# Fused attention and FFN on one core: all attention ahead of the first FFN product, with shared x and operand tiles

## The chip, the core and the metric

The kernel runs on one core of a Trainium2 chip. The core has a matrix engine (TensorE, PE in the profile, with its weight loads listed as PEld), a vector engine (VectorE, DVE), a scalar engine (ScalarE, ACT) and a queue that here only starts transfers (SyncE, SP). Matmuls write to PSUM, eight banks of 512 fp32 numbers on each of 128 partitions; all else lives in SBUF, 128 partitions wide. The metric is the device time of one execution in microseconds, the median of several runs. A profile is one execution recorded by the hardware.

## The reference

Attention with a sigmoid in place of the softmax, whose result is the input of a two-layer FFN with a leaky ReLU:

```python
def _attn_ref(q, k, v):                     # each 8 x 12 x 448 x 64, fp32
    S = q.shape[2]
    scale = 1.0 / np.sqrt(q.shape[-1])
    scores = scale * np.matmul(q, k.transpose(0, 1, 3, 2)) - np.log(S)
    attn = 1.0 / (1.0 + np.exp(-scores))
    return np.matmul(attn, v).astype(np.float32)

def _moe_ref(x, w_in, w_out):               # x: 3584 x 768, w_in: 768 x 2048, w_out: 2048 x 768
    h = x @ w_in
    g = np.maximum(0.01 * h, h)
    return (g @ w_out).astype(np.float32)
```

`x` is the attention output with its heads side by side. `moe_w_in` and `moe_w_out` come as float64 bits, read by the kernel as pairs of int32.

## The kernel before, in words

**Units of work.** A *pair* is two heads of one batch: 8 x 6 = 48 pairs, `pairs[0]` to `pairs[47]`. `scores(h)` does two of four chunks of keys (three matmuls for each chunk and head, since q and k are split into a high and a low fp32r part) and gives them to ScalarE's sigmoid; `attn_v(0)` and `attn_v(1)` multiply by v; `keep` copies the result from PSUM to a third of an `x` tile of [128, 3, 448]. A pair is of one of three kinds (`part`, line 42): kind 0 cuts its 448 keys into four chunks of 112; kinds 1 and 2 form a *couple*, each with three chunks of 128 keys and 64 keys left, and those last 64 of both lie in one tile, so that four 64 x 64 matmuls of attn·v for the two pairs stand where two times two of 112 rows did. Before, 22 couples and 4 pairs of kind 0 (`JOINT_ALONE`, `JOINT`, lines 36 and 37).

**The FFN.** Both products use a seven-product scheme: `ORDER = 0, 1, 4, 5, 3, 6, 2` (line 20). A *quarter* q is two batches, 12 pairs, four `x` tiles. From them come seven operands (`Operands`, line 435): x0, x1, two of them after sums in place (`s3`, `sum1`, `sum4`), and one sum tile s2. Each operand is split in a high part (cast on ScalarE) and a low part (subtraction on VectorE). The first product of a quarter (`First`, line 520) runs over eight units u and the seven operands: 56 *steps*, each nine matmuls of 128x128 by 128x448. After some steps `after` evacuates and sums PSUM on ScalarE and VectorE and stores the results g to DRAM. The second product, from line 743, reads g back.

**Weights.** `prep` (line 249) rebuilds 16 blocks of weights (eight of w_in, eight of w_out) on VectorE: for each piece five integer instructions, at the end four subtractions, then two stores to DRAM. It is a generator; `prepare(q)` advances it by `PACES` yields at each slot. The first four blocks come in two pieces of 128x768, through tiles of the operands' pool `so`, the others in four pieces of 128x384. `advance(t)` (line 501) handles the first product's prepared weights, four groups for each unit: load into one of three `stage` tiles up to eight steps ahead and at most three groups beyond the last low part, high part three steps ahead, low part two steps ahead.

**The order around the change.** Nearly all instructions are pinned to the order in which the program issues them, engine by engine. The program runs in *slots*: `later(n, f)` puts f into the slot n ahead, and `slot(work)` issues the chores of the slot, then its work. Quarter 0's pairs run alone (lines 639 to 658). Then, for q = 1 to 3, the first product of quarter q-1 runs with quarter q's 12 pairs inserted between its steps (lines 663 to 678): scores(0) of pair i, attn·v of pair i-1, scores(1) of pair i. The last quarter's product runs alone (line 686). `PLAN` and `PLAN_ALONE` (lines 483 to 490) say in which slot the operands' parts are made: "e5.0" is the first slot of the quarter's pair 5, "p50" step 50 of the quarter before, "np0" step 0 of its own product; "h002" is the high part of operand 0, thirds 0 to 2, "l" a low part, "s" a sum.

**Space.** Operands have eight tiles with room for both parts (`so`), x and s2 five (`xp`). In PSUM the scores have three double banks in quarter 0, two afterwards; attn·v has two banks; while product and pairs are mixed, the first product has one bank for `px` and one for `pz`. When it runs alone at the end it has three of each. Tiles of v come from the weights' `ring` for pairs 0 to 8 and from a pool of their own afterwards.

Of the kernel before, what the change touches and what calls it, by code (L numbers as in the profile page):

```python
# [26 lines left out]
ALONE = 4  # L27


PACES = 1.45, 2.45, 1.46  # L30
LATER = 4
IDLE = 7
WAIT = 2, 7


JOINT_ALONE = 1, 3, 5, 7
JOINT = 0, 2, 4, 6, 8, 10
PER = 12
AHEAD_OF = 3
# [19 lines left out]
def attn_ffn_kernel(ctx: ExitStack, tc: tile.TileContext, qk, v, w_in, w_out, out):  # L59
# [17 lines left out]
    KR = S // NK  # L77
# [9 lines left out]
    td = [[tc.dram_tile([P, NOP, HW], F32, name=f"t{w}_{u}") for u in range(NU)] for w in range(2)]  # L87
    gd = [[tc.dram_tile([P, NU, S], F32, name=f"g_{p}_{n}") for n in range(NOP)] for p in range(NQ)]
# [160 lines left out]
    def prep():  # L249
# [3 lines left out]
        pieces = [(m, k, 4 if m >= ALONE else 2) for m in range(len(todo)) for k in range(4 if m >= ALONE else 2)]  # L253
        raws = []

        def load():
            at = len(raws)
            if at == len(pieces):
                return
            m, k, n = pieces[at]  # L260
            w, u = todo[m]
            size = 4 * HW // n
            pool = (so, "so", 2 * NB * S, NOP + 1) if m < ALONE else (pp, "wr", 2 * HW, 3)
# [4 lines left out]
        load()  # L268
        load()
        yield  # L270
        for at, (m, k, n) in enumerate(pieces):
# [3 lines left out]
            if m < ALONE - 1:  # L275
                load()
            elif (m, k) == (ALONE - 1, 1):
                for _ in range(3):
                    load()
# [15 lines left out]
            if m >= ALONE:  # L295
                load()
                yield
# [11 lines left out]
            yield from (None for _ in range(WAIT[m >= ALONE]))  # L309
# [4 lines left out]
    def prepare(q):  # L314
        nonlocal credit
        credit += PACES[0] if q == 0 else PACES[1] if (0, NU - 1) not in prepared else PACES[2]
        while credit >= 1:
            next(preps, None)
            credit -= 1

    xs = {}

    HALVES = slice(0, S // 2), slice(S // 2, S)
    OTHERWISE = 9

    class Pair:
# [6 lines left out]
        def load_qk(self):  # L333
            self.raw = raws.tile([P, 2, S], F32, tag="qk", name=f"qk_{self.i}")
            if self.i == 0:

                for cols in HALVES:
                    dma_act(out=self.raw[:, 0, cols], in_=qk[self.i, :, 0, cols])
                    dma(out=self.raw[:, 1, cols], in_=qk[self.i, :, 1, cols])
            elif self.i == 1:  # L340
                dma_act(out=self.raw[:, 0], in_=qk[self.i, :, 0])
                dma(out=self.raw[:, 1], in_=qk[self.i, :, 1])
            else:
                dma(out=self.raw, in_=qk[self.i])

        def load_v(self):
            rows, n = ((KR, 2 * NK), (P, 2 * NK - 2), (P, 2 * NK))[self.part]
            if self.i < OTHERWISE:
                t = ring.tile([P, 4 * HW], F32, tag="ring", name=f"v_{self.i}")
                self.v = t[:, :2 * NK * D].rearrange("p (a b) -> p a b", a=2 * NK)  # L350
            else:
                self.v = raws.tile([P, 2 * NK, D], F32, tag="v", name=f"v_{self.i}", bufs=2)
            dma(out=self.v[:rows, :n], in_=v[self.i, :rows, :n])
# [8 lines left out]
        def split(self):  # L362
# [5 lines left out]
            for n, cols in enumerate(HALVES):  # L368
# [6 lines left out]
        def scores(self, h):  # L375
            todo, acts = [], []
            for c in range(2 * h, 2 * h + 2):
                ps = psum_s(self.i * NK + c, f"sc_{self.i}_{c}")

                if self.part == 0:  # L380
                    k0, n, rows = c * KR, KR, slice(0, KR)
                elif c < NK - 1:
# [26 lines left out]
        def attn_v(self, h):  # L409
            if h == 0:  # L410
                self.pv = psum_v("pv", f"pv_{self.i}")
            rows = slice(0, P if self.part else KR)
            for c in range(2 * h, 2 * h + 2):
                if self.part and c == NK - 1:
                    continue
                for j, me in enumerate(heads):
                    mm(self.pv[me, :S], lhsT=self.v[rows, (NK - 1 if self.part else NK) * j + c, :], rhs=self.a[c][rows, j],
                       start=c == 0, stop=c == NK - 1, skip_group_check=True)
            if h == 1 and self.part == 2:
# [5 lines left out]
                later(1, x.keep, first=True)  # L425
            if h == 1 and self.part != 1:
                later(1, self.keep, first=True)

        def keep(self):
            half, c = divmod(self.i, NB)  # L430
            if c == 0:
                xs[half] = xp.tile([P, NB, S], F32, tag="x", name=f"x_{half}")
            copy(out=xs[half][:, c], in_=self.pv[:, :S])

    class Operands:
# [3 lines left out]
        def __init__(self, p):  # L439
            self.p, self.t, self.s2 = p, {}, None  # L440
# [9 lines left out]
        def high(self, n, a=0, b=NB):  # L450
            if n not in self.t:
                self.t[n] = so.tile([P, 2, NB, S], F32R, tag="so", name=f"so{n}_{self.p}")
            copy(out=self.t[n][:, 0, a:b], in_=self.of(n)[:, a:b])

        def low(self, n, a=0, b=NB):
            sub(self.t[n][:, 1, a:b], self.of(n)[:, a:b], self.t[n][:, 0, a:b])

        def s3(self):
            sub(self.x(0), self.x(0), self.x(2))

        def sum2(self, a, b):
            if self.s2 is None:
                self.s2 = xp.tile([P, NB, S], F32, tag="x", name=f"s2_{self.p}")
            sub(self.s2[:, a:b], self.x(3)[:, a:b], self.x(0)[:, a:b])

        def sum1(self, a, b):
            add(self.x(2)[:, a:b], self.x(2)[:, a:b], self.x(3)[:, a:b])

        def sum4(self, a, b):
            sub(self.x(1)[:, a:b], self.x(1)[:, a:b], self.s2[:, a:b])  # L470

        def do(self, what):
# [3 lines left out]
            if kind == "s":  # L476
                self.s3() if n == 3 else (self.sum1 if n == 1 else self.sum2 if n == 2 else self.sum4)(a, b)
            else:
                (self.high if kind == "h" else self.low)(n, a, b)

    PLAN = {
# [3 lines left out]
    PLAN_ALONE = {  # L487
# [32 lines left out]
    class First:  # L520
# [6 lines left out]
        def step(self):  # L527
# [10 lines left out]
            x = self.ops.t[n]  # L538
            for kk in range(NB):
                parts_mm(acc, w, slice(kk * P, kk * P + P), x[:, 0, kk], x[:, 1, kk], first and kk == 0, kk == NB - 1)  # L540
# [38 lines left out]
    per = 2 * NP  # L579
# [5 lines left out]
    zeros = st.tile([P, S], F32, tag="st", name="zeros", bufs=ST)[:, :S // 4]  # L585
# [12 lines left out]
    first, ops = None, None  # L598
    psv = ExitStack()
    psum_v = banks("ps_v", dict(pv=(2, 1)), psv)  # L600
    psum_two = banks("ps_s", dict(s0=(1, 2), s1=(1, 2)), psv)
    psum = banks("ps_a", dict(s2=(1, 2)))

    def psum_s(n, name):

        if n < per * NK:
            return (psum if n % 3 == 2 else psum_two)(f"s{n % 3}", name)
        return psum_two(f"s{n % 2}", name)

    def next_parts(i, *slots, how=None):  # L610

        if i + 2 <= last:
            later(slots[0], lambda: pairs[i + 2].high(how))
            later(slots[1], pairs[i + 2].low)
        if i + 4 <= last:
            later(slots[2], pairs[i + 4].load_qk)

    def go(q, where, work, busy=False):


        for x, plan, key in ((ops, PLAN, where), (before, PLAN if q > 1 else PLAN_ALONE, "n" + where)):
            if x is not None:
# [210 lines left out]
```

## Time and profile before

| | us |
|---|---|
| median of 3 runs | 1105.76 (1105.23 to 1106.14) |
| the profiled execution | 1105.26 |
| its span, first to last instruction | 1103.5 |
| PE busy | 1094.4 |
| VectorE busy | 669.2 |
| ScalarE busy | 614.5 |
| mean granted TensorE clock | 0.998 of full speed |

The profile's names follow the program: `sc` are scores, `s` the sigmoid's results, `pv` attn·v in PSUM, `qk` and `qks` a pair's q and k and their parts, `so` operands, `wx`, `w` a staged weight and its parts, `px_h`, `py_h`, `pz_h` the first product's accumulators, the same with `_o` the second's, `wr`, `wd`, `ws` preparation of weights, `c_h` results of the first product. A row of the time line has start, length, engine, line, operation, output<-input, shapes and the number of instructions; in brackets stands the idle time before it and what ended it. Since every helper issues through one line, L92 says little, and the tile names tell the work. A row of a group has the busy time, the mean length of one in ns, and the idle time in front. A row of a stage has the busy time of PE, PEld, VectorE, ScalarE and GpSimd with the number of instructions, then the clock, the DMA engines' busy share and GB/s. Matmuls are pipelined, so the end of one overlaps the start of the next, and starts are more exact than lengths.

### The profile page before, as it was taken

To read this page: it belongs to the slowest core of one execution; us is meant where nothing else is said; L and a number is where in the kernel's file an instruction comes from. 1 tells how busy PE (TensorE), PEld (TensorE's weight loads), DVE (VectorE), ACT (ScalarE), POOL (GpSimd) and SP (SyncE) were. 2 spreads that over 40 slices of the span, in tenths; PEclk is the share of its full clock that TensorE was granted. 3 is DMA by queue.
4 is the path that set the end of the run, shared out by engine and by line. 5 is a ranking of instruction groups with operands and counts; after the bars stand their busy time and mean duration, and the time that the engine had idled before them with its cause. 6 is when DMAs were issued, how large, how long until landed. Compare 5 with 4: busy or idle time off the path is not lost.

```text
span 1103.5 us, 16033 instructions
## 1 busy us (share of the span) xinstructions
PE 1094.4 (99%) x5978; PEld 898.2 (81%) x5978; DVE 669.2 (61%) x998; ACT 614.5 (56%) x866; POOL 0.3 (0%) x5
## 2 busy tenths in 40 slices
PE   9998999999999999999999999999999999999998
PEld 5556777777777777777778999999999999999998
DVE  5888888668776678676568766565433333343332
ACT  7886676678666667665657555554333232323331
POOL 0000000000000000000000000000000000000000
PEclk9999999999999999999999999999999999999999
DMA  7966988885888876787755989777645554454452
GB/s 275 336 216 221 329 294 295 283 280 157 276 255 284 262 243 218 237 284 243 253 192 163 297 275 292 267 276 226 204 146 145 156 184 145 131 182 147 156 153 89
DMA packets 105422, 250.11 MB, mean 227 GB/s; under 512 B 11712, under 2 KB 55232, under 8 KB 105344
## 3 DMA queue, kind: packets, MB, share of 16 engines
q1 hardware_dynamic: 104912, 248.62, 68.5%
q8 instruction: 47, 0.77, 0.3%
q10 hardware_dynamic: 432, 0.46, 0.1%
q14 instruction: 31, 0.25, 0.1%
HBM read 164.63 MB, written 84.41 MB: 226 GB/s over the span
## 4 chain that ended last, share of the span: by engine, by line
PE 94%; DVE 3%; ACT 1%; DMA 1%; issue 1%; ACTq 0%; SPq 0%; DVEq 0%
PE px_h L92 21%; PE px_o L92 21%; PE pv L92 11%; PE pz_o L92 10%; PE pz_h L92 10%; PE sc L92 10%; PE py_h L92 5%; PE py_o L92 5%; DVE wd L92 1%; DVE so L92 1%; DVE qks L92 1%; DMA qk<-in_qk 0%; ACT s L92 0%; DMA v<-in_v 0%; ACT so L92 0%
## 5 line engine op out<-in xcount | busy, mean ns | idle before, releaser
L92 DVE TENSOR_TENSOR gs<-gg,gs 128x896 fp32r<-128x896 f32 x112 | 122.2, 1091 | 226.9 <-ACT gs L92 226.7
L92 PE MATMUL px_h<-so,w 128*128 128x448 f32 x1152 | 252.0, 367 | 3.1 <-DVE c_h L92 3.1
L92 PEld LDWEIGHTS px_h<-so,w 128*128 128x128 f32 x1152 | 214.9, 189 | 28.9 <-issue 12.8
L92 PE MATMUL px_o<-gs,w 128*128 128x448 f32 x1152 | 232.5, 362 | 0.0
L92 ACT CAST gs<-gg 128x896 fp32r<-128x896 f32 x112 | 105.5, 943 | 223.1 <-PE px_o L92 116.2
L92 PEld LDWEIGHTS px_o<-gs,w 128*128 128x128 f32 x1152 | 216.2, 188 | 14.2
L92 ACT ACTIVATE s<-sc 128x896 f32<-128x896 f32 (+1 forms) x192 | 171.6, 918 | 71.0 <-PE sc L92 47.8
L92 DVE TENSOR_TENSOR w<-wx,w 128x768 fp32r<-128x768 f32 (+1 forms) x160 | 136.1, 852 | 15.9 <-ACT w L92 15.5
L92 PEld LDWEIGHTS sc<-qks 64*128 64x128 f32 (+2 forms) x1164 | 97.8, 179 | 57.6 <-issue 27.5
L92 PE MATMUL sc<-qks 64*128 64x448 f32 (+3 forms) x1164 | 142.6, 380 | 1.1 <-DVE qks L92 0.6
L92 PE MATMUL pv<-s,v 128*64 128x448 f32 (+2 forms) x768 | 141.9, 551 | 0.2 <-DMA v<-in_v 0.2
L92 PE MATMUL pz_h<-so,w 128*128 128x448 f32 x576 | 126.1, 363 | 0.0
L92 ACT CAST w<-wx 128x768 fp32r<-128x768 f32 (+1 forms) x160 | 119.7, 751 | 5.1 <-DMA wx<-t 4.8
L92 PE MATMUL pz_o<-gs,w 128*128 128x448 f32 x576 | 116.5, 362 | 0.0
L92 PEld LDWEIGHTS pz_h<-so,w 128*128 128x128 f32 x576 | 107.8, 188 | 8.2 <-issue 0.7
L92 PEld LDWEIGHTS pz_o<-gs,w 128*128 128x128 f32 x576 | 108.1, 188 | 7.1
L92 PEld LDWEIGHTS pv<-s,v 128*64 128x64 f32 (+2 forms) x768 | 42.8, 135 | 76.9 <-issue 75.4
L92 DVE TENSOR_TENSOR qks<-qk,qks 128x896 fp32r<-128x896 f32 (+1 forms) x51 | 52.7, 1034 | 33.1 <-ACT qks L92 32.8
L92 DVE SCALAR_TENSOR_TENSOR wd<-wr,wd 128x384 int32<-128x384 int32 (+1 forms) x112 | 68.7, 613 | 2.7
L92 ACT COPY c_h<-px_h 128x448 f32<-128x448 f32 x64 | 34.1, 532 | 61.2 <-PE px_h L92 57.9
L92 ACT ACTIVATE c_h<-c_h 128x448 f32<-128x448 f32 x96 | 55.2, 575 | 19.6 <-DVE c_h L92 19.5
L92 PE MATMUL py_h<-so,w 128*128 128x448 f32 x288 | 62.9, 363 | 0.0
(41 smaller groups left out, 670.4 us busy)
## 6 DMA issues: line engine op xcount, KB each, us to landing
gg<-g SPq DMA_DIRECT2D x112, 448.0 KB, 3.5
wx<-t SPq DMA_DIRECT2D x120, 384.0 KB, 4.2
g<-c_h SPq DMA_DIRECT2D x128, 224.0 KB, 4.8
g<-s SPq DMA_DIRECT2D x96, 224.0 KB, 4.6
qk<-in_qk SPq DMA_DIRECT2D x46, 448.0 KB, 5.3
t<-ws SPq DMA_DIRECT2D x16, 768.0 KB, 5.1
wr<-in_w_out SPq DMA_DIRECT2D x32, 384.0 KB, 4.7
out<-c_o SPq DMA_DIRECT2D x48, 224.0 KB, 2.0
```

What stands on the lines that cost most here:

```text
L92: return lambda *args, **kw: tc.keep_in_program_order(issue(*args, **kw))
```

## The change

- `part(i)` is now `1 + i % 2`: 24 couples, no pair of kind 0. The first pair's keys are cut at 256 instead of 224 for its first loads and splits.
- The loop over quarters with inserted pairs is gone. All 48 pairs run first, one after the other; then the four quarters' first products, 56 steps each; then the second product as before.
- PSUM: in attention three double banks for scores and two for attn·v; in the first product three banks each for `px` and `pz` throughout.
- x tiles, s2 and the operands' parts (high and low now in tiles of their own, [128, 3, 448] each) share 24 tiles, 10 on the left side of SBUF and 14 on the right, and five more once attention's pools are closed. `take` hands out the tile given back longest ago; `give` returns one.
- The last quarter's x doesn't stay in SBUF: `keep` copies it to one of two `xo` tiles and stores that to DRAM (`xd`); at steps 0 to 3 of quarter 2's product four loads bring it back (`PLAN_LAST`).
- `PLAN_ATTN` makes quarter 0's operands during pairs 13 to 41; in the pairs where a high part is made on ScalarE, the q/k cast of pair j + 2 goes to VectorE. `PLAN` makes the other quarters' operands during the product of the quarter before and the first steps of their own.
- Preparation of weights has four pieces for every block and a pace of 2.2 yields a slot in attention, and 2 yields at steps 7 to 48 of the first three products where the step's number modulo 7 is 6, 0, 1 or 2.
- `EARLY` says in which slots of the last pairs the first product's weights are loaded and split.
- All tiles of v come from `ring`.

```diff
-PACES = 1.45, 2.45, 1.46
+PACES = 2.2, 2
+WAIT = 7
...
+LEFT, MORE, RIGHT = 10, 5, 14
 def part(i):
-    q, j = divmod(i, PER)
-    firsts = JOINT if q else JOINT_ALONE
-    return 1 if j in firsts else 2 if j - 1 in firsts else 0
+    return 1 + i % 2
...
+    xd = [tc.dram_tile([P, NB, S], F32, name=f"xd_{n}") for n in range(4)]
...
+    free = {"left": [], "right": []}
+    def tiles(stack, name, side, n):
+        pool = stack.enter_context(tc.tile_pool(name=name, bufs=1, side=side, reuse_waits="tile"))
+        free[side].extend((pool, f"{name}{i}", side) for i in range(n))
+    taken = {}
+    def take(name, dtype, sides=("right", "left")):
+        place = next(free[side] for side in sides if free[side]).pop(0)
+        pool, tag, _ = place
+        t = pool.tile([P, NB, S], dtype, tag=tag, name=name)
+        taken[name] = place
+        return t
+    def give(name):
+        place = taken.pop(name)
+        free[place[2]].append(place)
...
-    so = left.enter_context(tc.tile_pool(name="so", bufs=NOP + 1))
-    st = left.enter_context(tc.tile_pool(name="st", bufs=ST))
+    tiles(left, "l", "left", LEFT)
+    attn = ExitStack()
+    raws, spl, at, xo = (attn.enter_context(tc.tile_pool(name=name, bufs=bufs, reuse_waits="tile")) for name, bufs in (
+        ("raws", 2), ("spl", 2), ("at", 5), ("xo", 2)))
-    xp, pp, raws, spl, at = (right.enter_context(tc.tile_pool(name=name, bufs=bufs, side="right")) for name, bufs in (
-        ("xp", 5), ("pp", 2), ("raws", 2), ("spl", 2), ("at", 5)))
+    tiles(right, "r", "right", RIGHT)
+    pp = right.enter_context(tc.tile_pool(name="pp", bufs=2, side="right"))
...
         def keep(self):
             half, c = divmod(self.i, NB)
+            if half >= KEPT:
+                t = xo.tile([P, S], F32, tag="xo", name=f"xo_{self.i}")
+                copy(out=t, in_=self.pv[:, :S])
+                dma(out=xd[half - KEPT][:, c], in_=t)
+                return
             if c == 0:
-                xs[half] = xp.tile([P, NB, S], F32, tag="x", name=f"x_{half}")
+                xs[half] = take(f"x_{half}", F32)
             copy(out=xs[half][:, c], in_=self.pv[:, :S])
...
+        def high(self, n, a, b):
+            if n not in self.hi:
+                self.hi[n] = take(f"hi{n}_{self.p}", F32R, self.sides)
+            copy(out=self.hi[n][:, a:b], in_=self.of(n)[:, a:b])
+        def low(self, n, a, b):
+            if n not in self.lo:
+                self.lo[n] = take(f"lo{n}_{self.p}", F32R, self.sides)
+            sub(self.lo[n][:, a:b], self.of(n)[:, a:b], self.hi[n][:, a:b])
+            if b == NB and n not in (0, 1):
+                give(f"s2_{self.p}" if n == 4 else f"x_{4 * self.p + {5: 0, 3: 2, 6: 3, 2: 1}[n]}")
+        def used(self, n):
+            give(f"hi{n}_{self.p}")
+            give(f"lo{n}_{self.p}")
+        def load(self, n, a, b):
+            i = 4 * self.p + n
+            xs[i] = take(f"x_{i}", F32)
+            dma(out=xs[i], in_=xd[n])
...
+    PLAN_ATTN = {
+        "e13.1": "h002", "e15.1": "l002", "e17.1": "h102", "e19.1": "l102", "e20.1": "s302", "e22.1": "s202", "e24.1": "s402",
+        "e26.1": "s102", "e27.1": "h402", "e29.1": "l402", "e30.1": "h502", "e32.1": "l502", "e33.1": "h302", "e35.1": "l302",
+        "e36.1": "h602", "e38.1": "l602", "e39.1": "h202", "e41.1": "l202"}
     PLAN = {
+        "p12": "h002", "p13": "l002", "p14": "s302", "p19": "h102", "p20": "l102", "p21": "s202", "p27": "s402", "p28": "s102",
+        "p33": "h402", "p34": "l402", "p50": "h502", "p51": "l502", "p54": "h302", "p55": "l302 h602", "np0": "l602",
+        "np2": "h202", "np3": "l202"}
+    PLAN_LAST = dict(PLAN, p0="x002", p1="x102", p2="x202", p3="x302")
...
+    EARLY = {(-4, 0): -8, (-4, 2): -6, (-3, 0): -4, (-2, 0): -3, (-1, 0): -2, (-1, 2): -1, (0, 0): 0}
...
+    psum = banks("ps_a", dict(s=(3, 2), pv=(2, 1)))
...
+    for j in range(last + 1):
+        works = [lambda: pairs[j].scores(1)] + [lambda: pairs[j + 1].scores(0)] * (j < last)
+        works += [lambda: pairs[j].attn_v(0), lambda: pairs[j].attn_v(1)]
+        if j + 2 <= last:
+            later(0, pairs[j + 2].load_v)
+            later(1, lambda j=j: pairs[j + 2].high(vcopy if PLAN_ATTN.get(f"e{j}.1", "").startswith("h") else copy))
+            later(2, pairs[j + 2].low)
+        if j + 4 <= last:
+            later(4, pairs[j + 4].load_qk)
+        for n, work in enumerate(works):
+            go([(ops[0], PLAN_ATTN.get(f"e{j}.{n}", ""))], work, PACES[0] * (j > 0))
+            t = EARLY.get((j - last, n))
+            if t is not None:
+                advance(t)
...
+    ps.close()
+    attn.close()
+    st = left.enter_context(tc.tile_pool(name="st", bufs=ST, reuse_waits="tile"))
+    tiles(left, "m", "left", MORE)
+    psum = banks("ps_f", dict(px=(3, 1), pz=(3, 1)))
+    size = NU * NOP
+    def product(q, first, k):
+        todo = []
+        for x, key in ((q, f"np{k}"), (q + 1, f"p{k}")):
+            if 0 < x < NQ:
+                todo.append((ops[x], (PLAN if x < NQ - 1 else PLAN_LAST).get(key, "")))
+        go(todo, first.step, PACES[1] * (7 <= k < size - 7 and k % 7 in (6, 0, 1, 2)))
+    for q in range(NQ - 1):
+        first = First(q, ops[q])
         for k in range(size):
+            product(q, first, k)
...
+    first = First(NQ - 1, ops[-1])
+    for k in range(NOP):
+        product(NQ - 1, first, k)
```

More of the change, by code (lines that the diff above doesn't have):

```diff
@@ L266, in load @@
             raws.append(raw)
-        load()
-        load()
+        for _ in range(3):
+            load()
         yield
-        for at, (m, k, n) in enumerate(pieces):
+        for at, (m, k) in enumerate(pieces):
             w, u = todo[m]
@@ L294, in prep @@
             yield
[L295 to L297 removed]
+            load()
+            yield
             if k < n - 1:
@@ L410, in attn_v @@
             if h == 0:
[L411 to L415, printed above, removed]
+                self.pv = psum("pv", f"pv_{self.i}")
+            for c in range(2 * h, min(2 * h + 2, NK - 1)):
                 for j, me in enumerate(heads):
-                    mm(self.pv[me, :S], lhsT=self.v[rows, (NK - 1 if self.part else NK) * j + c, :], rhs=self.a[c][rows, j],
-                       start=c == 0, stop=c == NK - 1, skip_group_check=True)
+                    mm(self.pv[me, :S], lhsT=self.v[:, (NK - 1) * j + c, :], rhs=self.a[c][:, j], start=c == 0, stop=False,
+                       skip_group_check=True)
             if h == 1 and self.part == 2:
@@ new lines, in sum @@
+        def sum(self, n, a, b):
+            if n == 2 and self.s2 is None:
+                self.s2 = take(f"s2_{self.p}", F32)
+            to, fn, x, y = {
+                3: (self.x(0), sub, self.x(0), self.x(2)),
+                2: (self.s2, sub, self.x(3), self.x(0)),
+                1: (self.x(2), add, self.x(2), self.x(3)),
+                4: (self.x(1), sub, self.x(1), self.s2)}[n]
+            fn(to[:, a:b], x[:, a:b], y[:, a:b])
+            if b == NB:
+                self.got.add(n)
@@ L597, in attn_ffn_kernel @@
     pairs[3].load_qk()
[L598 to L616, printed above, removed]
@@ L679, in attn_ffn_kernel, with go @@
-    ps.close()
-    psv.close()
-    KS = 2
-    assert next(preps, None) is None
-    psum = banks("ps_f", dict(px=(3, 1), pz=(3, 1)))
-    for k in range(NOP):
-        go(NQ, f"p{k}", first.step, True)
-    right.close()
+    ops = [Operands(q) for q in range(NQ)]
+    psum = banks("ps_a", dict(s=(3, 2), pv=(2, 1)))
+    def go(todo, work, pace=0):
+        for x, what in todo:
+            for y in what.split():
+                later(0, lambda x=x, y=y: x.do(y))
+        slot(work)
+        prepare(pace)
@@ new lines, in attn_ffn_kernel @@
+    unread = psum("s", "unread")[:, 0]
+    for _ in range(IDLE):
+        mm(unread[heads[0], :S // 4], lhsT=zeros[:, :D], rhs=zeros, start=True, stop=True)
+    slot(lambda: pairs[0].scores(0))
+    for j in range(last + 1):
[12 more added lines that the diff above has]
+                advance(t)
@@ L717, in attn_ffn_kernel @@
     w2 = {(g, u): Weights(1, u, g, t2a, "t2", None, g_tile) for g, u in use[:AHEAD]}
-    for k in range(NOP, NU * NOP):
+    for k in range(NOP, size):
         m, at = divmod(k - NOP, 6)
```

159 lines of the change are left out of this document (37 added, 122 removed), and 6 rows, old and new, of tables (PLAN, PLAN_ALONE).

## The prediction

> **What bounds the kernel now.** First the page: span, busy times, and the shares of its chain of work.
>
> ```profile
> span 1103.5 us, 16033 instructions
> ...
> PE 1094.4 (99%) x5978; PEld 898.2 (81%) x5978; DVE 669.2 (61%) x998; ACT 614.5 (56%) x866; POOL 0.3 (0%) x5
> ...
> PE 94%; DVE 3%; ACT 1%; DMA 1%; issue 1%; ACTq 0%; SPq 0%; DVEq 0%
> ```
>
> TensorE (PE) is the chain, so a change is worth what it does to PE's own time or to its few waits. The profiled run took 1105.26 us, 1.76 more than its span and 0.5 under the median of 1105.76. The next question is how long the same matmuls take in each setting. The second view is PE's time line (start, length, tile, count). A group's last matmuls overlap the next group, so I take start to start. First attention alone, then attention mixed with the first FFN product:
>
> ```profile
> 10.22 3.23 PE L92 MATMUL pv<-s,v 112*64 112x448 f32 x16
> 13.37 2.83 PE L92 MATMUL sc<-qks 64*128 64x448 f32 x24
> 16.13 2.48 PE L92 MATMUL pv<-s,v 128*64 128x448 f32 x12
> 18.54 2.82 PE L92 MATMUL sc<-qks 64*128 64x448 f32 x24
> 21.28 3.39 PE L92 MATMUL pv<-s,v 128*64 128x448 f32 x20
> 24.60 2.84 PE L92 MATMUL sc<-qks 64*128 64x448 f32 x24
> 27.37 2.48 PE L92 MATMUL pv<-s,v 128*64 128x448 f32 x12
> ...
> 243.50 1.49 PE L92 MATMUL sc<-qks 64*128 64x448 f32 x12
> 244.92 3.39 PE L92 MATMUL pv<-s,v 128*64 128x448 f32 x20
> 248.24 1.48 PE L92 MATMUL sc<-qks 64*128 64x448 f32 x12
> 249.65 2.08 PE L92 MATMUL px_h<-so,w 128*128 128x448 f32 x9
> 251.56 1.96 PE L92 MATMUL pz_h<-so,w 128*128 128x448 f32 x9
> ...
> 258.86 1.48 PE L92 MATMUL sc<-qks 64*128 64x448 f32 x12
> ...
> 264.10 1.08 PE L92 MATMUL px_h<-so,w 128*128 128x448 f32 x4
> ```
>
> Alone, a couple (two pairs that share a chunk of last keys) runs from 16.13 to 27.37: **11.24 us**, that is pv 2.41 + 3.32 and two sc of 2.755; half a pair's scores (12 matmuls) is 1.378. A pair outside a couple has a pv of 3.15 (10.22 to 13.37). Now the chain in the product alone, PE's one long wait, and the first starts of both products:
>
> ```profile
> 603.07 1.80 PE px_h L92 x9
> ...
> 696.67 14.40 PE px_o L92 x72
> ```
> ```profile
> 78.39 2.08 PE L92 MATMUL px_h<-so,w 128*128 128x448 f32 x9
> ...
> 98.06 5.44 PE L92 MATMUL px_h<-so,w 128*128 128x448 f32 x18 [3.14 <-DVE c_h L92]
> ```
>
> A product step (9 matmuls) is **1.80 us**. In the mixed part, 243.50 to 258.86 holds one pair and five steps: 15.36 - 5 x 1.80 = 6.36. The next pair takes 264.10 - 258.86 = 5.24, and the step behind it loses the 0.21 that the five steps from 249.65 to 258.86 lost (9.21 for 9.00): 5.45. A mixed couple is thus **11.81 us**: 0.57 more than alone, of which 0.42 are two restarts of the product. At 98.06 PE has waited 3.14, and its next 18 matmuls take 5.44 where two steps take 3.60: 1.84 more, 5.0 in all.
>
> Check: 78.39 + 224 steps x 1.80 (403.2) + 18 mixed couples x 11.81 (212.6) - scores of pair 12, already done (2.8) + 5.0 = 696.4; the second product begins at 696.67. The price list holds to 0.3 us.
>
> **The change, part by part.**
>
> *Attention in front.* All 48 pairs run alone, in 24 couples. The first pv stays at 10.22 (the start differs by keys cut 256/192 for 224/224 and three weight loads of half the size for two; perhaps 0.2 either way). Then 24 x (2.41 + 3.32) = 137.5; score halves: 96 less 3 that lie earlier, 93 x 1.378 = 128.2; one restart, 0.2. The first product begins at 276.1 and ends 403.2 later, at 679.3. The second product and the tail aren't touched: 1103.5 - 696.7 = 406.8. Sum **1086.1 us of span**, 1087.9 of time if nothing waits, 17.4 less. By cause: mixing 18 x 0.57 = 10.3; two more couples 2 x (2 x 3.15 - 5.73) = 1.1; the wait at 98.06, 5.0; 0.9 in small waits of today's attention (67.3 by the list, 78.39 - 10.22 = 68.17 in fact). The wait at 98.06 is for an add that frees the only px bank, late in the queue of VectorE (DVE) behind weight preparation and operands; with three banks each for px and pz a step needs a bank that was freed a unit ago, so nothing of that kind is next.
>
> *Does attention stay PE's?* Stages of the trace (busy PE, PEld, DVE, ACT, POOL; clock, DMA share, GB/s), and durations (busy, mean ns):
>
> ```profile
> 10.22:78.39 68.17, 67.65 (x471) 34.11 (x469) 54.66 (x73) 57.72 (x74) 0.00 (x0) 1.00 0.82 297
> 614.90:665.30 50.40, 50.40 (x253) 47.30 (x253) 33.63 (x51) 28.56 (x51) 0.00 (x0) 1.00 0.86 285
> ```
> ```profile
> L92 DVE TENSOR_TENSOR w<-wx,w 128x768 fp32r<-128x768 f32 x120 | 114.0, 952 | 10.1 <-ACT w L92 10.0
> L92 ACT ACTIVATE s<-sc 128x896 f32<-128x896 f32 x132 | 120.3, 920 | 67.9 <-PE sc L92 46.0 <-PE pv L92 21.3 <-ACT x L92 0.2
> L92 ACT CAST w<-wx 128x768 fp32r<-128x768 f32 x120 | 99.4, 833 | 5.1 <-DMA wx<-t 4.8
> L92 DVE SCALAR_TENSOR_TENSOR wd<-wr,wd 128x384 int32<-128x384 int32 x96 | 53.4, 556 | 2.2
> L92 DVE TENSOR_TENSOR qks<-qk,qks 128x896 fp32r<-128x896 f32 x47 | 51.2, 1089 | 32.9 <-ACT qks L92 32.8
> L92 ACT CAST qks<-qk 128x896 fp32r<-128x896 f32 x42 | 39.4, 939 | 0.1
> L92 DVE TENSOR_TENSOR so<-x,so 128x1344 fp32r<-128x1344 f32 x21 | 32.6, 1555 | 2.8 <-ACT so L92 2.5
> L92 ACT CAST so<-x 128x1344 fp32r<-128x1344 f32 x21 | 27.6, 1316 | 2.4 <-DVE x L92 1.3 <-DVE wd L92 1.0
> L92 ACT COPY x<-pv 128x448 f32<-128x448 f32 x48 | 23.5, 537 | 24.7 <-PE pv L92 24.6
> L92 DVE TENSOR_TENSOR c_h<-c_h,py_h 128x448 f32<-128x448 f32 x32 | 19.8, 620 | 33.0 <-PE py_h L92 21.8 <-ACT qks L92 5.5 <-ACT w L92 5.0
> L92 DVE TENSOR_TENSOR ws<-wd 128x384 f32<-128x384 f32 x32 | 17.7, 552 | 0.1
> L92 DVE TENSOR_SCALAR wd<-wd 128x384 f32<-128x384 f32 x48 | 17.2, 358 | 1.1
> ```
> ```profile
> 38.28 0.88 PE L92 MATMUL sc<-qks 64*128 64x448 f32 x6 [0.35 <-ACT s L92]
> ```
>
> ScalarE (ACT) per pair: 4 x 0.92 + 0.94 + 0.54 = 5.16 of 5.62. The seven casts of the first operands (1.32) fall on pairs whose q/k cast goes to DVE: 5.54, covered, barely. Today the first such cast, beside a q/k cast, cost the 0.35 at 38.28. Bounds 0 to 7 x 0.5; I take **0.7**, 0.1 each, since the q/k cast makes room. DVE per pair: a block of weights is 4 x (3 x 0.358 + 2 x 0.556) + 4 x 0.552 = 10.95 over 35 yields; four slots at 2.2 yields make 2.75, the low part of q/k 1.09: 3.84 of 5.62, with 1.55 for an operand now and then. Covered; without that slack scores would wait for their low parts, one for one. The last 12 pairs' x goes out on SP behind its copy; the q/k and v loads queued behind it have two pairs of lead (11 us): nothing. The first product's operands are ready by pair 41, its first weights are cast at pair 45: nothing at the join. Traffic: about 0.69 MB of q, k and v and a quarter of a block's 2.95 MB in 5.62 us, 254 GB/s, under the 297 of the row.
>
> *The product alone.* Today the last product runs alone with no PE wait at 33.63 of 50.40 for DVE, about 29 of it without the second product's first weights (4.7 x 0.95): 7.3 in the 12.6 us of a unit (seven steps). New beside it, in three products: 48 yields each (15.0) and 11 operand instructions of 1.55 (17.1): 8 x 7.3 + 32.1 = 90.5 of 100.8, **90% of DVE**. Its tightest place is from the add at step 6 of a unit to the low weights of step 4 in the next, five steps or 9.0 us later (units 2, 3, 4): two adds from PSUM and two sums (4 x 0.62), an operand's low part and a sum (2 x 1.555), two weight parts (2 x 0.95), six yields (2.2): 9.7. Back to back, DVE does better than its means:
>
> ```profile
> 618.10 1.82 DVE L92 TENSOR_TENSOR w<-wx,w 128x768 fp32r<-128x768 f32 x2
> ```
>
> That is 1.82 for two of 0.95, 0.08 less; over eight of these 0.65: 9.05. So 0 to 0.7 at each of nine places, 0 to 6.3 in all. Low weights are read from a step's third matmul on (0.4 later), so I take 0.2 each, **1.8**. Behind a late low part its stage tile's next load waits on SP, and the saves behind that load. ACT gains 7 x 1.32 a product on 57%; its casts into tiles just given back wait a step at most: covered.
>
> *x from DRAM.* Four loads of 672 KB on SP at steps 0 to 3 of the third product, among the weights: 2.75 MB in 7.2 us, on top of a stage near 250 GB/s (285 less the second product's weights). Landing times of weights, issues from 600 to 690 us and the whole trace:
>
> ```profile
> wx<-t SPq DMA_DIRECT2D x26, 384.0 KB, 4.8
> ```
> ```profile
> DMA to landing us min/median/max: 2.3/3.8/10.8
> ```
>
> A weight group has 7 to 8 steps from issue to need, about 8 us of it for landing, so a landing of 10.8 would cost 3 once. I take **0.5**.
>
> Sum 1086.1 + 0.7 + 1.8 + 0.5 = 1089.1 of span, 1090.9 of time.
>
> **Two rules of the skill.** The Trainium skill, Perfetto Trace Analysis, Optimization Strategy: where the most contended engine differs between regimes, interleaving these may gain; taking attention out would then lose. Here attention alone is PE's too (67.65 of 68.17), so the trace doesn't agree; by the rule it would go as in the third rival. The Trainium skill, TensorE: Matmul & The Clock Gate, HAM oscillation: idle gaps above about 3.4 us lower the clock; the row at 98.06 has the slow matmuls after 3.14 already.
>
> **Rivals.**
>
> 1. *DVE is late in the first three products*, 90% busy with adds in its queue that wait for PE. For: 9.05 to 9.7 against 9.0. Against: units 5 to 7 are lighter, so it recovers. Price: 9 x 0.7 for my 1.8, and one wait of the kind at 98.06 (5.0) on top in the bad case: 1095 to 1100.
>
> 2. *Slower: the three stage tiles of weights.* A tile's round is landing + cast 0.83 + low part 0.95. Four groups in 12.6 us on three tiles allow 9.45 a round, so weights set the pace from a mean landing of 7.7. Each further us adds 4/3 a unit, 32 over 24 units; the kernel is slower than before from 8.2. At 8.6: +29, 1120. For: 250 GB/s, and 40 more for preparation. Against: the row from 614.90 has 285 GB/s and no PE wait, with landings of 4.8.
>
> 3. *Attention alone doesn't keep the pace of its first 68 us*; ACT, DVE and SP are late by turns. At 5.90 a pair, today's mixed rate, 48 x 0.28 = 13.4 goes back: 1104, no difference. Against: ACT and DVE, with 85% and 80% there, carry no more per pair than now.
>
> **How the numbers follow.** The forecast has 0.73 (1087 to 1095), rival 1 0.18, rival 3 0.04, rival 2 0.05. I predict **1090.9 us**. The range **1087 to 1099** leaves out rivals 2 and 3 and the end of rival 1. A measurement of this kernel tells apart about 0.2%, 2.2 us: faster 0.92, same 0.03, slower 0.05.
>
> **What would show it.** The first product begins near 276 and runs in steps of 1.80 with no restarts of 0.21; the second begins near 682. Rival 1: PE waits for DVE w in units 2 to 4; rival 2: ACT waits for DMA wx throughout; rival 3: the first product begins past 285. The prediction is wrong if attention takes over 5.7 a pair, or if PE waits more than 6 us in the product.

## The result, and the profile after

| | before | after |
|---|---|---|
| median, us | 1105.49 (1105.16 to 1106.14, 4 runs) | 1092.59 (1089.91 to 1095.69, 4 runs) |
| ratio, 95% interval | | 0.9884 (0.9856 to 0.9911) |
| profiled execution, us | 1105.26 | 1095.69 |
| its span, us | 1103.5 | 1093.5 |

The kernel is 1.2% faster, 12.9 us. It was forecast at 1090.9 in a range of 1087 to 1099. Its runs now lie 6 us apart, where those of the kernel before lie within 1 (in the later measurements within 3, 1103.45 to 1106.39). The profiled one is the slowest of the four.

First PE's time line of the kernel after: start, length, tile, count. Attention begins and settles, then hands over to the first product.

```profile
9.64 2.48 PE L85 MATMUL pv<-s,v 128*64 128x448 f32 x12
12.05 2.82 PE L85 MATMUL sc<-qks 64*128 64x448 f32 x24
14.80 3.39 PE L85 MATMUL pv<-s,v 128*64 128x448 f32 x20
18.11 2.84 PE L85 MATMUL sc<-qks 64*128 64x448 f32 x24
20.88 2.48 PE L85 MATMUL pv<-s,v 128*64 128x448 f32 x12
...
272.37 3.39 PE L85 MATMUL pv<-s,v 128*64 128x448 f32 x20
275.69 0.47 PE L85 MATMUL px_h<-hi,w 128*128 128x448 f32 x1
```

A couple still takes 11.24 (9.64 to 20.88). Attention ends after 275.69 - 9.64 = 266.05; the price list says 137.5 + 128.2 = 265.7, so casts, preparation and stores of x cost it about 0.4 at most. The first pv comes 0.58 earlier than before.

Now the chain of work of the same kernel (start, length, what), where it leaves PE, and where the second product begins.

```profile
494.58 0.42 SPq L85
495.01 0.05 issue
495.06 5.72 DMA g<-s
500.77 0.02 issue
500.80 0.64 DVE s L85
501.44 0.53 ACT c_h L85
501.96 0.04 issue
502.01 3.73 PE px_h L85 x9
505.74 2.77 PE pz_h L85 x9
508.51 3.60 PE px_h L85 x18
...
686.71 14.40 PE px_o L85 x72
```

From 275.69 to 686.71 the four products take 411.0 where 224 steps are 403.2. (In PE's time line the second product starts at 686.55, which makes 410.9; the runs below are read that way.) PE stands until 502.01, and two steps behind that take 6.50 (502.01 to 508.51) where two take 3.60. Read from the matmul upwards, PE waited for ScalarE, ScalarE for a sum on VectorE, and the sum for a **store** of an earlier result: its tile was still being read. What led to the store's late issue at 495.06 stands in the time lines of SP, ScalarE and VectorE (the brackets have the idle time before and what ended it):

```profile
489.19 5.34 SPq L85 DMA_DIRECT2D wx<-t  x2
494.58 0.42 SPq L85 DMA_DIRECT2D wr<-in_w_out  x1
495.06 0.42 SPq L85 DMA_DIRECT2D g<-s  x1
```
```profile
492.36 0.83 ACT L85 CAST w<-wx 128x768 fp32r<-128x768 f32 x1 [3.45 <-DMA wx<-t]
```
```profile
493.23 0.96 DVE L85 TENSOR_TENSOR w<-wx,w 128x768 fp32r<-128x768 f32 x1 [2.12 <-ACT w L85]
...
500.80 0.63 DVE L85 TENSOR_TENSOR s<-s,c_h 128x448 f32<-128x448 f32 x1 [3.90 <-DMA g<-s]
```

A weight group lands late, just after the four x loads. Its cast waits 3.45 for it, its low part is done at 494.2, and only then can SP issue the second of the two wx loads of the first row, since that one writes to the stage tile which the low part frees. The store of g stands behind it in SP's queue. The second product shows the same at the same step, smaller:

```profile
397.11 0.48 PE L85 MATMUL px_h<-hi,w 128*128 128x448 f32 x1 [0.55 <-ACT c_h L85]
```

The first product begins at 275.69, the second and third 56 steps later each (about 376.5 and 477.6), so both waits come at the step numbered 11. What the two have in common, and the first product has not, is a product before it, whose last unit has its sums and stores delayed by `LATER = 4` steps into the first steps of the next. (So has the fourth product, which shows no such wait; it has neither x loads nor preparation of weights beside it.)

### The profile page after: what moved, and what is told of

It is laid out like the page before. It is cut to its first block, busy times and chain, and to the rows that moved or that the text cites. A ratio compares the mean times of both kernels' runs of the same rounds, so it can differ in the third digit from the quotient of the medians.

```text
span 1093.5 us, 16196 instructions
## 1 busy us (share of the span) xinstructions
PE 1084.4 (99%) x5978; PEld 900.1 (82%) x5978; DVE 678.2 (62%) x1022; ACT 608.6 (56%) x855; POOL 0.3 (0%) x5
## 4 chain that ended last, share of the span: by engine, by line
PE 54%; DMA 1%; ACT 0%; DVE 0%; SPq 0%; issue 0%
PE px_o L85 21%; PE pz_o L85 11%; PE px_h L85 10%; PE py_o L85 5%; PE pz_h L85 5%; PE py_h L85 2%; DMA g<-s 1%; DVE s L85 0%; ACT c_o L85 0%; ACT c_h L85 0%; SPq L85 0%
## 5 line engine op out<-in xcount | busy, mean ns | idle before, releaser
L85 PE MATMUL px_h<-hi,w 128*128 128x448 f32 x768 | 233.0, 364 | 4.1 <-ACT c_h L85 4.1
L85 ACT ACTIVATE s<-sc 128x896 f32<-128x896 f32 x192 | 167.9, 917 | 26.7 <-PE sc L85 25.0
L85 PEld LDWEIGHTS px_h<-hi,w 128*128 128x128 f32 x768 | 144.6, 188 | 16.1 <-ACT c_h L85 5.0
L85 PEld LDWEIGHTS sc<-qks 64*128 64x128 f32 (+1 forms) x1164 | 97.8, 180 | 55.6 <-ACT s L85 29.0
L85 PE MATMUL pv<-s,v 128*64 128x448 f32 (+1 forms) x768 | 140.7, 551 | 0.0
L85 PE MATMUL px_h<-lo,w 128*128 128x448 f32 x384 | 139.8, 364 | 0.0
L85 PE MATMUL sc<-qks 64*128 64x448 f32 (+2 forms) x1164 | 137.4, 379 | 0.4 <-ACT qks L85 0.3
L85 ACT CAST w<-wx 128x768 fp32r<-128x768 f32 (+1 forms) x160 | 119.7, 751 | 17.2 <-DMA wx<-t 17.1
L85 PE MATMUL pz_h<-hi,w 128*128 128x448 f32 x384 | 118.8, 364 | 0.0
L85 PEld LDWEIGHTS pz_h<-hi,w 128*128 128x128 f32 x384 | 72.7, 189 | 5.1
L85 PEld LDWEIGHTS px_h<-lo,w 128*128 128x128 f32 x384 | 72.5, 189 | 4.5
```

What stands on the lines that cost most here:

```text
L85: return lambda *args, **kw: tc.keep_in_program_order(issue(*args, **kw))
```

## The experiments

Three theories. **A**: the x loads make weights land late, and SP's order hands this on to the stores. **B**: VectorE, which has preparation to do in the product (85.86 of the 101 us of the second one), is late by itself (the prediction's first rival). **C**: the nine tiles of results are too few while the delayed sums of the last unit hold some, with or without x.

**x loads spread out.**

```diff
-    PLAN_LAST = dict(PLAN, p0="x002", p1="x102", p2="x202", p3="x302")
+    PLAN_LAST = dict(PLAN, p1="x002", p4="x202", p8="x102", p12="h002 x302")
```

> The four loads of x from DRAM start at steps 1, 4, 8 and 12 of the third product instead of 0, 1, 2 and 3; nothing else moves. Theory A (the four x loads crowd the weights and stores; a weight group lands late, SP's next load waits for the late low part, a store of g behind it lands late and a sum waits for that store's tile): PE's wait of 3.55 us at step 11 of the third product falls below 1, the clock stays full, the first product takes about 404.5 instead of 411.0, time about 1089, the runs within 1 us of each other. Theory B (VectorE, busy with preparation, is late by itself): the wait stays above 2.5 and the time near 1092. Theory C (the nine tiles of results are too few after the delayed sums of a product's last unit, with or without x): the wait falls only to the 0.55 that the second product shows, time about 1089.5.

Measured 1090.99 (1090.43 to 1092.40), ratio 0.9875 (0.9860 to 0.9889). The product takes 683.5 - 277.0 = 406.5. PE's time line in this run, the rows with a wait in the third product:

```profile
500.48 0.47 PE L85 MATMUL px_h<-hi,w 128*128 128x448 f32 x1 [0.91 <-ACT c_h L85]
...
503.37 0.47 PE L85 MATMUL pz_h<-hi,w 128*128 128x448 f32 x1 [0.80 <-ACT c_h L85]
```

The 3.55 became 0.91 and 0.80 and the clock stayed full, which speaks against B. It is weak evidence: A had the wait below 1 and the product at 404.5, and the spreads of this run and of the changed kernel overlap. An execution of the unaltered changed kernel, further down, has a product of 406.6 too.

**Eleven tiles of results.**

```diff
-ST = 9
+ST = 11
-            pool = pp, "wr", 2 * HW, 3
+            pool = pp, "wr", 2 * HW, 2
-        for _ in range(3):
+        for _ in range(2):
```

> Eleven tiles for the first product's results instead of nine; to make room, preparation has two pieces of raw weights in flight instead of three. Theories A and C: ScalarE still waits about 3 us for a weight load in the third product, but no sum waits for a store, so PE waits under 0.5 in both the second and the third product; time 1088 to 1089. Theory B: PE's wait at step 11 of the third product stays above 2.5; time near 1092. If two pieces are too few for preparation, VectorE waits for raw weights and attention gets longer than 266.1 us.

Measured 1088.84 (1088.19 to 1089.50), ratio 0.9853 (0.9839 to 0.9868). The product takes 679.7 - 275.9 = 403.8. The waits of PE in this run, all of them, and one of ScalarE (total us, times, longest):

```profile
PE unread L85 <- DVE zeros L612: 1.0, 1, 1.0
PE sc L85 <- ACT qks L85: 0.3, 1, 0.3
PE sc L85 <- DVE qks L85: 0.2, 1, 0.2
```
```profile
ACT w L85 <- DMA wx<-t: 17.5, 15, 2.7
```

ScalarE waits for weight loads as long as in the changed kernel (17.1 there), and PE waits for nothing in the product. Late weights alone cost nothing; the tile of the sum made the cost. This speaks for C, and against B, as preparation had the same work to do, though with one piece less of raw weights in flight.

**Sums not delayed.**

```diff
-LATER = 4
+LATER = 0
```

> The sums and stores of each product's last unit aren't delayed by four steps (in the fourth product's last unit as well). Theory C: the store that the sum at step 11 waits for goes out earlier, the 0.55 in the second product goes and the wait in the third falls below 1.5; time 1088.5 to 1090. Theory A: the wait in the third product stays above 2.5. Price: VectorE has two sums more in the first steps of a product beside two low parts of operands; at most 1 us a product.

Measured **1088.12** (1087.91 to 1088.26), ratio 0.9847 (0.9831 to 0.9863): the fastest version, and its four runs lie within 0.4. The product takes 679.1 - 275.6 = 403.5. Its VectorE still waits 3.15 at the same place, for a cast that waits for a load, and the sums find their tiles free:

```profile
492.24 0.96 DVE L85 TENSOR_TENSOR w<-wx,w 128x768 fp32r<-128x768 f32 x1 [3.15 <-ACT w L85]
...
495.11 0.62 DVE L85 TENSOR_TENSOR s<-s,c_h 128x448 f32<-128x448 f32 x1
```

The row at 495.11 is the sum that waited until 500.80. So the part of C that names the delayed sums holds: without the delay, the x loads, where they were, are free. The expected price of the undelayed sums, up to 1 us a product, didn't come.

**x loads one product earlier.** Is x then only a bystander?

```diff
-    PLAN_LAST = dict(PLAN, p0="x002", p1="x102", p2="x202", p3="x302")
+    PLAN_LAST = PLAN
+    LOADS = dict(p0="x002", p1="x102", p2="x202", p3="x302")
...
+        if q == 1:
+            todo.append((ops[3], LOADS.get(f"p{k}", "")))
```

> The changed kernel, with the four x loads at steps 0 to 3 of the second product instead of the third. Theory A+C (x loads and delayed sums together make the wait at step 11): PE's wait at step 11 of the second product grows from 0.55 to 2 to 4 us with slow matmuls behind it, that of the third falls to 0.5 or less; time about 1092. Theory C alone (x has no part in it): both waits stay as they were, 0.55 and about 3.5. Theory B: the third keeps its wait, since its preparation is where it was.

Measured 1090.89 (1090.25 to 1091.87), ratio 0.9873 (0.9858 to 0.9887). PE's time line and its waits in this run:

```profile
398.75 0.48 PE L85 MATMUL px_h<-hi,w 128*128 128x448 f32 x1 [2.59 <-ACT c_h L85]
```
```profile
PE px_h L85 <- ACT c_h L85: 2.9, 2, 2.6
```

The large wait went along with the loads, from the third product to the second (0.55 to 2.59), and 0.3 is left for the other. So A and C are both needed, and C's "with or without x" is wrong: the delayed sums leave a sum without a spare tile, and x traffic turns that from half a microsecond to three. That the traffic does it by way of SP's order is read from the time lines; no run moves the store to another queue. The slow matmuls that were expected behind the wait didn't come, see the last section.

**The changed kernel again.**

> The changed kernel once more, unaltered, beside the others on one chip: 1090 to 1096, with PE's wait at step 11 of the third product between 1 and 4 us. If its spread comes from that wait, runs of it differ by several us where the runs with undelayed sums lay within 0.4.

Measured 1092.29 (1090.46 to 1095.26). Its profiled run, of 1091.29, has 2.2 as PE's longest wait and 682.4 - 275.8 = 406.6 for the product. Over the 1088.12 of the undelayed sums that run has 3.2, and over its 403.5 the product has 3.1. For the first profiled run, of 1095.69, the same differences are 7.6 and 7.4. So in both executions with a trace the time above the undelayed version lies in the product, and this wait, with the slow matmuls behind it in one of them, makes most of it (2.2, and 3.55 with 2.90). The other executions have no trace; that their spread is this wait too is likely, not shown.

**Preparation all in attention.** Would the product have been free without VectorE's load, and can attention take it?

```diff
-PACES = 2.2, 2
+PACES = 3.0, 0
```

> All preparation of weights lies in attention (3.0 yields a slot, none in the product). Theory B: every wait of PE in the product goes, 403.4 for the four products. Theory A: the wait at step 11 of the third product stays above 2, since x still crowds the loads, though raw weights and prepared blocks are no longer in the way. VectorE per pair in attention: 12 yields (3.75) + 1.09 = 4.84 of 5.62, 6.4 where an operand's 1.55 falls, and DMA about 305 GB/s: attention grows by 0 to 6 us from 266.1. Time 1088 to 1095.

Measured 1107.30 (1105.40 to 1114.79), ratio 1.0028 (1.0011 to 1.0045). The product begins at 294.6 and takes 698.1 - 294.6 = 403.5, with no wait of PE, although the x loads, the delayed sums and the nine tiles are those of the changed kernel. Theory A, which had the wait stay above 2, failed here, and A and C together aren't enough either: by this one traced execution the wait needs preparation in the product as a third thing. VectorE alone, as B has it, isn't the cause, since the runs with eleven tiles and with undelayed sums kept preparation in the product and had no wait. Whether preparation acts by VectorE's time or by its own loads and stores, no run separates. The price was that attention lost 18.9 us, three times the most I expected. Stage 10 to 276 us in this run (PE, PEld, VectorE, ScalarE, GpSimd, clock, DMA share, GB/s), and its waits from 10 to 270:

```profile
10.00:276.00 266.00, 254.84 (x1776) 128.42 (x1778) 220.33 (x423) 214.38 (x267) 0.00 (x0) 0.99 0.84 288
```
```profile
DVE wd L85 <- DMA t<-wd: 15.3, 7, 4.2
...
PE sc L85 <- DVE qks L85: 9.8, 11, 1.7
ACT qks L85 <- DMA qk<-in_qk: 9.2, 8, 1.7
```

VectorE stands at tiles whose store is under way (15.3), the low parts of q and k stand behind it, and PE waits for those.

> All preparation in attention again, with fourteen empty yields after each block instead of seven and 3.6 yields a slot instead of 3.0, so that the work per pair is the same but a block's stores have twice the pause before their tile is written again; sums undelayed. If the 19 us that attention lost came from VectorE standing at a tile whose store was under way, with the q and k parts queued behind it, most of that goes: attention 266 to 272. Rival (VectorE hasn't the time, whatever the order): attention 280 or more.

```diff
-PACES = 2.2, 2
-WAIT = 7
+PACES = 3.6, 0
+WAIT = 14
-LATER = 4
+LATER = 0
```

Measured 1105.46 in one run; the product begins at 293.4. The waits for stores halved, and of the 18.9 us only 1.2 came back: attention takes 283.7 (from the first pv at 9.69), near the rival's 280 or more.

```profile
PE sc L85 <- DVE qks L85: 10.5, 11, 2.8
ACT qks L85 <- DMA qk<-in_qk: 8.0, 11, 2.2
DVE wd L85 <- DMA t<-wd: 7.7, 7, 1.6
DVE qks L85 <- DMA qk<-in_qk: 7.4, 5, 1.8
```

Now the waits for q and k loads have grown. VectorE is 83% busy in both runs (73% in the undelayed one, 193.17 of 266), and DMA moves 288 to 290 GB/s. Which of the two sets the limit stays open, so the rival's number came and its cause isn't shown.

**The price list on the kernel before: its one long wait.**

```diff
-    def prepare(q):
+    def prepare(q, pace=None):
...
-            prepare(q)
+            prepare(q, 0.8 if q == 1 and where.startswith('e1.') else None)
```

> The kernel before, with preparation of weights slowed to 0.8 yields a slot (2.45 before) in the four slots of pair 13, right where VectorE was late for PE's one long wait; about six yields (3 us of VectorE) come later. If that wait of 3.14 and the slow matmuls behind it (1.84) are worth 5.0, the time is about 1100.7 and TensorE has no wait over 0.5 in the first product. Rival: VectorE is late at that place because of the operands, and the wait stays above 2; time 1103 or more.

Measured **1100.44** (1100.38 to 1101.60), ratio 0.9961 (0.9946 to 0.9976). No PE wait above 0.6, and at the place of the long wait the steps run on:

```profile
92.81 1.96 PE L92 MATMUL pz_h<-so,w 128*128 128x448 f32 x9
94.61 3.76 PE L92 MATMUL px_h<-so,w 128*128 128x448 f32 x18
98.21 1.96 PE L92 MATMUL py_h<-so,w 128*128 128x448 f32 x9
```

The kernel before, measured beside it, had 1105.29. So 4.8 us of the change's gain needed none of it, only a slower pace of preparation over four slots.

**Four pairs outside couples**, with undelayed sums: the code for four chunks of 112 keys is put back, and

```diff
-    return 1 + i % 2
+    return 0 if i < 4 else 1 + i % 2
```

> Undelayed sums (as in the run with no delay), and pairs 0 to 3 outside couples (four chunks of 112 keys each), 22 couples as in the kernel before. By the price list each two of these cost 2 x 3.15 - 5.73 = 0.57 more of attn.v: the first product begins 1.1 us later than without it, time 1089.2. Rival: the couples' 64 x 64 matmuls give nothing that the kernel keeps, 1088.1.

Measured 1090.37 (1089.54 to 1091.44), ratio 0.9871 (0.9854 to 0.9887). First pv and first product in this run:

```profile
10.02 3.23 PE L86 MATMUL pv<-s,v 112*64 112x448 f32 x16
...
277.18 0.47 PE L86 MATMUL px_h<-hi,w 128*128 128x448 f32 x1
```

From the one to the other 267.16; the run with undelayed sums has 9.59 to 275.60, 266.01. That is 1.15 for two couples less, and the list has 1.14. The first pv comes 0.4 later, and with that the two profiled executions are explained: 1089.54 and 1087.99 are 1.55 apart. The medians are 2.2 apart, and the rest lies in executions without a trace.

**Fewer switches on the kernel before** (on the version with no long wait): eight of a quarter's pairs stand two by two.

```diff
-        places = {round(j * spread[0] / per) - spread[1]: j for j in range(q > 1, per + 1)}
+        places = {}
+        for j in range(q > 1, per + 1):
+            place = j + (j % 2 == 0 and 0 < j < per - 2)
+            places.setdefault(round(place * spread[0] / per) - spread[1], []).append(j)
         for k in range(size):
-            j = places.get(k)
-            if j is not None:
+            for j in places.get(k, ()):
```

> The kernel before without its long wait (as in that run, 1100.4), and in each quarter eight of the mixed pairs stand two by two between steps of the first product, at four places instead of eight: 12 switches between attention and the product fewer. By the price list each saves a restart of 0.21 and some of the 0.07 that half a pair's scores cost more when cut off: 2.5 to 3.4 in all, time 1097.0 to 1098.0. Rival: the switch costs nothing by itself and the 0.57 of a mixed couple lies elsewhere: 1100.4, or more, as scores of two pairs in a row wait for the sigmoid with two double banks.

Measured 1110.10 (1109.73 to 1110.40), ratio 1.0046 (1.0029 to 1.0062): 9.7 slower than the version it is built on (the kernel before had 1105.18 and 1105.29 beside the two). The forecast failed, by the mechanism that the rival named. The chain of work over one group in this run:

```profile
281.38 3.39 PE pv L92 x20
284.77 0.95 ACT x L92 x2
285.72 0.83 ACT s L92
286.55 0.04 issue
286.60 1.65 PE sc L92 x12
288.24 2.41 PE pv L92 x12
290.65 1.42 PE sc L92 x12
292.06 2.01 PE px_h L92 x9
294.07 1.80 PE pz_h L92 x9
```

There is now one restart (2.01 for 1.80) for two pairs, as the list has it, but between the pairs PE waits for a bank: ScalarE copies two x, then does the sigmoid that frees it. PE still has scores to do for most of that time and stands for 0.49 of it; over the run there are 13 waits for a sigmoid, 6.1 us in all. In the mixed part the scores have two double banks, alone they have three. The time of this run therefore doesn't price the switch, and its part of the 0.57 rests on the time lines.

## Why the prediction was right, and where it was not

*Attention in front, the floor.* Right. The prediction's sum with no waits was 1086.1 of span; the version with undelayed sums, whose product has none, has 1086.2 and 1088.12 of time (1087.9 predicted). That it fits to 0.1 is partly luck: the first pv came 0.6 earlier than assumed, and attention (0.3), the product (0.1) and what follows it (0.3) took that back. By parts: couples alone 11.24 as before; the wait 5.0, measured 4.8; mixing 10.3, couples 1.1 and small waits 0.9, together 12.3, and 1100.44 - 1088.12 is 12.3. Of these the couples were measured by themselves (1.15). The 10.3 of mixing was not: it is what remains, with the earlier start and the new banks in it, and agrees with the couples' lengths in the time lines.

*Casts in attention*, 0.7. Too high: 0.4 or less.

*VectorE in the product*, 1.8, and the first rival. The load was sized a little high (90% forecast, 85.86 of 101 us in the second product), and the tight places cost nothing: with the tiles free, PE never waits for a low part. The term should have been 0.

*x from DRAM*, 0.5. This term failed, in its size and in its mechanism. I priced it as weights that land late and bounded it by what PE needs of weights; PE never waited for weights. The prediction said that behind a late low part the next load waits on SP "and the saves behind that load", and left it there: it didn't ask who waits for the saves. The answer was a sum in need of a result tile, with PE behind its evacuation: 7.4 us in the profiled run, some 4.5 in the median (1092.59 against 1088.12). The kernel before delays the same sums into its last product without such a wait, but that product has neither x loads nor preparation beside it, and the runs show that the large wait needs both.

*The total.* 1090.9 was 1.7 below the median, and that is partly luck: the terms for casts and VectorE were 2.1 or more too high together, and the term for x 4.0 too low.

*Rival 2*, three stage tiles, didn't happen: casts waited 17.1 us for loads in all, and by themselves such waits cost PE nothing (17.5 with eleven tiles). *Rival 3* didn't happen at 2.2 yields; at 3.0 it does. The prediction called this covered because VectorE had 3.84 of 5.62 to do for a pair, with something over for an operand. Measured, VectorE is busy 73% of attention at 2.2 yields, and at 83% the pace is lost: the room was less than the idle share, whether VectorE or the transfers beside it set the limit.

Of the rules named in the prediction: the Trainium skill, Perfetto Trace Analysis, Optimization Strategy, says that interleaving may help where the most contended engine changes between regimes. Here it is PE in both, so the rule doesn't apply, and the runs go the other way: interleaved without its long wait 1100.44, apart and with undelayed sums 1088.12.

## What to carry to other kernels

When PE is the bound, price the same matmuls in each neighbourhood from start to start; the list that reproduces the old span to 0.3 us gave the new floor to 0.1, partly because small errors cancelled. When a transfer becomes late, follow its issue queue past the first instruction that waits: the store behind it, the tile that this store holds, and who needs the tile. One wait can have three causes that cost little without each other: here late sums, x loads and preparation of weights. A time that varies more after a change than before it can be a sign of such a wait: removing one delay of four steps gave 4.5 us and narrowed the runs from 6 us to 0.4.

## What the runs showed of the hardware that was not expected

Whether a wait of PE slows the matmuls behind it. Behind the wait of 3.14 us in the kernel before, two steps took 5.44 instead of 3.60, and behind that of 3.55 in the changed kernel 6.50. The stage around the latter has a granted clock of 0.83:

```profile
490.00:510.00 20.00, 16.45 (x69) 14.67 (x69) 11.75 (x21) 8.09 (x13) 0.00 (x0) 0.83 0.82 279
```

Behind 2.59 (x loads one product earlier) the matmuls ran at full speed: 398.75 to 402.47 is two steps in 3.72, at a granted clock of 1.00 from 390 to 410 us. Behind 2.18 (the changed kernel again) the clock stayed full too. That looks like a limit on the length of a wait, between 2.6 and 3.1. But in the run with all preparation in attention, a wait of only 1.72 has slow matmuls behind it, 20 of attn·v in 5.08 where they take 3.39:

```profile
153.26 1.28 PE L85 MATMUL sc<-qks 64*128 64x448 f32 x10 [1.72 <-DVE qks L85]
154.47 5.08 PE L85 MATMUL pv<-s,v 128*64 128x448 f32 x20
```

So the length of a wait alone doesn't decide it. What fits all twelve traces is where the wait falls. In the traces' records of the granted clock, its changes lie on a grid of 3.41 us that starts with the first change to full clock: in the kernel before that is at 5.90, and the clock is halved from 98.06 to 101.47, which is 27 and 28 periods later. Four traces have such a halving between their first and last matmul, and in the period just before it PE stood for 3.14, 2.41, 2.34 and 1.72 us. In no other period did PE stand for more than 1.62. The waits of 2.59 and 2.18 were cut in two by the end of a period, into 1.17 and 1.42, and 0.89 and 1.29. This was worked out after the runs, and no run was made to test it. It doesn't say why the clock stayed halved for two periods in the changed kernel (500.87 to 507.70) and for one in the other three.

If it holds, the same wait costs more in one execution than in the next. The kernel before points that way: of its 27 executions beside the experiments, the eight with a mean granted clock of 0.999 or 1.000 took 1103.45 to 1104.56, the others 1104.99 to 1106.81. The Trainium skill, TensorE: Matmul & The Clock Gate, HAM oscillation, puts the limit at about 3.4 us of idleness; here 1.72 us was enough once, and 2.59 was not.
